# A new order for a whole kernel: retention with SwiGLU on one core, the first chunk in an older order

## The chip, the cores and the metric

The kernel runs on one core of a Trainium2 chip. A core has TensorE (PE, matrix products; its weight loads are shown as PEld), VectorE (DVE), ScalarE (ACT), GpSimd (POOL) and SyncE (SP, which only issues DMAs here); each runs its own queue of instructions in order, and they wait for each other by semaphores. Times are device microseconds (us). The metric is the median time of several executions; a profile is taken of one of them.

## The reference

Two parts, one after the other. First a retention layer with a state that decays by a factor of its own in each head, over 4 batches, 8 heads, 768 positions and 64 dimensions per head; then RMS norm and a SwiGLU layer over the 3072 rows of 512 that come out.

```python
gamma = 1.0 - 2.0 ** (-5.0 - np.arange(H))
for t in range(S):
    state = gamma * state + einsum('bhd,bhe->bhde', k[:, :, t], v[:, :, t])
    y[:, :, t] = scale * einsum('bhd,bhde->bhe', q[:, :, t], state)
x = y.transpose(0, 2, 1, 3).reshape(B * S, H * D)
xn = x / sqrt(mean(x * x, -1) + 1e-06) * rms_g            # 3072 x 512
g = xn @ w_gate                                           # 512 x 1536
out = (g * sigmoid(g) * (xn @ w_val)) @ w_out             # 1536 x 512
```

Inputs and output are float32; the kernel computes in bfloat16 with float32 sums.

## The kernel before

The 768 positions are six chunks (c = 0 to 5) of 128; a chunk has four batches (b = 0 to 3). For each (c, b) the retention is: load q, k, v; transpose q and k; scores by two groups of products, for the even and the odd heads (`A`, line 414); multiply each half by a decay mask on VectorE (`M0`, `M1`, line 437); products with v, and from chunk 1 on with the state as well (`Y`, lines 452 and 456); squares summed on ScalarE (`S`, line 469); 1/rms on GpSimd, two instructions (`R`, lines 479 and 481: ms and rstd); the norm on VectorE (`N`, line 493); transposition of the normed rows into xnT, by TensorE and a copy (`X`, `XE`) in chunks 0 and 1 and by a DMA from SyncE (`XE` on S) later. The state of the next chunk is made by `D` (k times decay, line 528, chunks 0 and 1), `K` (products, line 537), `U` (sum, line 545, or copy) and `B` (two casts on GpSimd, line 552).

The feed-forward part takes the four batches of a chunk together, 512 columns of xnT: for each 128 of the 1536 hidden columns `g` and `v` (line 560, four products each, into one bank of PSUM each), `s` (silu on ScalarE, line 570) and `h` (their product on VectorE, line 582). In chunk 0 the first of these are cut by batch: `g.0.2.3.0.3` is chunk 0, hidden block 2 to 3, batches 0 to 3. The output product is done by seven products per chunk instead of eight: `a1`, `a6`, `a7`, `a4`, `b2`, `c5`, `c3` (line 656), with sums of hT made ahead of them (`z1` to `z4`, line 629, on VectorE or GpSimd), sums of w_out (`w1` to `w4`, line 614), partial results kept (`q1`, `q6`, `q7`) and added (`r1` to `r4`, line 679 or a copy at line 148), and stores (`s1` to `s4`, line 684).

Nothing of the order is left to a scheduler: a table of some 985 entries, `ORDER`, is read from first to last, and each entry issues one step.

```python
for w in ORDER.split():
    w, _, bk = w.partition("/")        # the PSUM banks it takes
    w, _, en = w.partition("@")        # the engine: D, A, P, S
    f, *a = w.split(".")               # the step and its chunk, batch, blocks
    F[f](ENG.get(en), [int(i) for i in bk], *map(int, a))
```

So an entry sets the engine, the banks and the place in that engine's queue; each engine runs its own entries in the order of the table, and runs ahead of the others as far as data and buffers allow.

Loads (`Lq`, `Lk`, `Lv`; line 313) on GpSimd (@P) turn float32 into bfloat16 on the way. Those of q and k of chunk 0 on GpSimd take eight rows of a head at a time (line 323) and are transposed by sixteen small products with the tile `pick` (`T`, line 377); all others take rows (line 325) and need four transposes (line 382). For the former, k in rows is got back by transposing once more (`J`, line 521). Loads on SyncE (@S) arrive as float32 and are copied or scaled (`Ck`, `Cq`, `V`), and from chunk 2 on q and k are transposed by DMAs from SyncE (`tq`, `tk`, line 398). All loads of chunk 2 wait for the transfer wo.8.12, the last third of w_out:

```python
        if c == 2:
            after(i, ("wo", 8))
```

Weights come in by pieces on GpSimd (`wg`, `wv`, line 334; `wo`, line 341): wv.4.6 is blocks 4 and 5 of w_val. Warm-up products on a tile of ones (`hot`, line 242; `H`, line 248, 512 wide) stand in the head. Constants are made there too: `iota` (row_m), `ident`, `pick`, the masks `mk0`, `mk1`, `vd`, `yd`, `yt` on ScalarE, `causal`, `mc`, and `rms`, `G`, `GE` for the norm's weights; `tab` loads ScalarE's table for silu.

Of the kernel before, what the change touches and what calls it, by code (L numbers as in the profile page):

```python
# [22 lines left out]
M1.0.1 M0.0.1 K.0.3/4 Y.0.0/7 S.0.0 Y.0.1/2 R.0.3 A.0.2/63 J.0.2/5 N.0.3 wv.0.2 wv.2.4 M0.0.2 K.0.1/0 M1.0.2 Y.0.2/1
wg.4.6 S.0.1 H.3/6 R.0.1 D.0.2@D K.0.2/3 R.0.0 N.0.0 N.0.1 Tk.1.1/5 U.0.1@A U.0.2@D X.0.3/0 U.0.3@A S.0.2 Lq.1.0@P
R.0.2 Tk.1.2/4 Lk.1.0@P mc.0@P Tq.1.2/7 tab Ek.1.1@A N.0.2 Tk.1.3/6 XE.0.3@A Ek.1.2@D Eq.1.2@D Lq.1.1@P X.0.1/2
X.0.0/3 Tq.1.3/5 XE.0.1@A X.0.2/1 g.0.0.4.3.4/0 A.1.2/47 g.0.0.2.1.2/2 XE.0.0@D Eq.1.3@D XE.0.2@A g.0.3.4.0.3/3
v.0.0.4.3.4/5 s.0.0.4.3.4 mc.1@P M1.1.2 v.0.3.4.0.3/1 M0.1.2 v.0.0.2.1.2/0 h.0.0.4.3.4 D.1.3@D v.0.2.3.0.3/7 Ek.1.3@A
A.1.3/64 s.0.0.2.1.2 h.0.0.2.1.2 g.0.0.2.2.3/2 s.0.3.4.0.3 h.0.3.4.0.3 M0.1.3 M1.1.3 g.0.0.2.0.1/3 s.0.0.2.0.1
g.0.2.3.0.3/5 Tk.1.0/0 Ek.1.0@D wv.4.6 s.0.2.3.0.3 h.0.2.3.0.3 v.0.0.2.0.1/1 Tq.1.0/6 g.0.5.6.0.3/3 s.0.5.6.0.3 B.0.2
Eq.1.0@D v.0.5.6.0.3/4 h.0.5.6.0.3 Tq.1.1/5 D.1.0@D Eq.1.1@D h.0.0.2.0.1 g.0.4.6.3.4/0 g.0.4.5.0.3/7 s.0.4.5.0.3  # L30
s.0.4.6.3.4 v.0.0.2.2.3/6 v.0.4.5.0.3/3 h.0.4.5.0.3 s.0.0.2.2.3 h.0.0.2.2.3 wg.9.12 wv.9.12 Lv.1.2@P g.0.9.10.0.4/4
D.1.2@P wg.6.9 B.0.3 A.1.0/5701 M1.1.0 Lv.1.0@P Lv.1.1@P Lv.1.3@P v.0.4.6.3.4/2 h.0.4.6.3.4 wo.0.4 v.0.10.11.0.4/3
M0.1.0 g.0.10.11.0.4/6 wo.4.8 Y.1.2/7 D.1.1@P s.0.9.10.0.4 S.1.2 v.0.9.10.0.4/4 s.0.10.11.0.4 g.0.7.8.0.4/2
s.0.7.8.0.4 z1.0.0@D M1.1.1 K.1.2/5 M0.1.1 h.0.9.10.0.4 B.0.1 B.0.0 wo.8.12 Lq.2.0@S R.1.2 N.1.2 Y.1.1/1 S.1.1 Y.1.0/0
S.1.0 h.0.10.11.0.4 R.1.1 K.1.1/6 U.1.1@D g.0.6.7.0.4/4 U.1.2@D Lq.2.3@S Lq.2.2@S Lk.2.3@S R.1.0 Lv.2.3@S Lk.2.0@S
Y.1.3/7 s.0.6.7.0.4 S.1.3 R.1.3 N.1.1 N.1.0 K.1.0/2 U.1.0@D wv.6.9 g.0.8.9.0.4/3 X.1.2/6 z2.0.0@P w1@P v.0.11.12.0.4/5
Cq.2.3@P X.1.1/4 X.1.0/1 z4.0.0@P g.0.11.12.0.4/0 K.1.3/2 XE.1.2@D Lk.2.2@S XE.1.1@A Cq.2.2@P Ck.2.3@P s.0.11.12.0.4
N.1.3 X.1.3/6 XE.1.0@D g.1.3.4.0.3/7 v.1.2.3.0.3/4 v.1.1.2.0.3/1 v.1.3.4.0.3/0 Cq.2.0@P XE.1.3@D h.0.11.12.0.4 tq.2.2
U.1.3@D s.1.3.4.0.3 h.1.3.4.0.3 g.1.9.10.0.4/6 g.1.0.4.3.4/5 v.1.9.10.0.4/2 s.1.9.10.0.4 h.1.9.10.0.4 g.1.2.3.0.3/7
v.0.6.7.0.4/0 h.0.6.7.0.4 g.1.6.7.0.4/6 s.0.8.9.0.4 g.1.1.2.0.3/2 v.0.7.8.0.4/3 Ck.2.2@P Lv.2.0@S s.1.2.3.0.3  # L40
h.1.2.3.0.3 tk.2.3 B.1.3 h.0.7.8.0.4 z1.0.1@D v.0.8.9.0.4/0 g.1.8.9.0.4/7 s.1.6.7.0.4 s.1.8.9.0.4 g.1.5.6.0.4/4
Lk.2.1@S tq.2.3 z3.0.0@D h.0.8.9.0.4 s.1.1.2.0.3 z2.0.1@D v.1.0.1.0.3/6 Ck.2.1@P h.1.1.2.0.3 z1.0.2@D z3.0.2@D
z2.0.2@D z3.0.1@P B.1.2 z4.0.2@D w2@D v.1.8.9.0.4/3 h.1.8.9.0.4 g.1.0.1.0.3/0 s.1.0.1.0.3 v.1.0.4.3.4/7 V.2.0@A
Ck.2.0@A tk.2.2 v.1.6.7.0.4/2 Lv.2.2@S g.1.4.5.0.4/1 h.1.0.1.0.3 w3@D v.1.4.5.0.4/0 h.1.6.7.0.4 s.1.0.4.3.4
h.1.0.4.3.4 s.1.4.5.0.4 s.1.5.6.0.4 g.1.7.8.0.4/3 v.1.5.6.0.4/6 h.1.5.6.0.4 Lq.2.1@S Cq.2.1@D h.1.4.5.0.4 s.1.7.8.0.4
v.1.7.8.0.4/5 h.1.7.8.0.4 a1.0.0.3/1 A.2.2/2743 q1.0@D M0.2.3 B.1.1 g.1.11.12.0.4/6 tq.2.0 Lk.3.2@S s.1.11.12.0.4
g.1.10.11.0.4/0 V.2.2@P K.2.2/5 tk.2.0 B.1.0 a6.0.0.3 tk.2.1 v.1.11.12.0.4/4 s.1.10.11.0.4 M1.2.3 V.2.3@D U.2.2@D
M0.2.2 Y.2.3/6 q6.0@A Ck.3.2@A tq.2.1 A.2.0/3052 S.2.3 Lv.3.3@S V.3.3@A z4.0.1@P w4@P M1.2.2 Y.2.2/7 B.2.2 R.2.3
h.1.11.12.0.4 a7.0.0.3 Lv.2.1@S V.2.1@P Lk.3.1@S M0.2.0 S.2.2 M0.2.1 M1.2.0 c5.0.0.3/4 Y.2.0/3 Lq.3.3@S R.2.2 S.2.0
v.1.10.11.0.4/5 M1.2.1 N.2.3 Y.2.1/0 Lq.3.0@S R.2.0 q7.0@A Lq.4.0@S Lk.3.3@S K.2.1/2 b2.0.0.3/6 a4.0.0.3 S.2.1 r4.0@A  # L50
XE.2.3@S Ck.3.1@D N.2.2 K.2.3/7 r2.0 c3.0.0.3 N.2.0 h.1.10.11.0.4 R.2.1 N.2.1 Cq.3.3@P U.2.3@D z1.1.1@P z2.1.1@D
z4.1.1@D r1.0 Lv.3.2@S U.2.1@D a1.1.0.3/3 XE.2.2@S B.2.1 XE.2.0@S XE.2.1@S z1.1.2@D V.3.2@D Cq.3.0@P K.2.0/5 U.2.0@D
# [674 lines left out]
```

## Time and profile before

| | |
|---|---|
| runs, us | 235.49, 237.01, 237.24 (median 237.01) |
| the profiled execution, us | 236.33; its span, from the first to the last instruction, 234.5 |
| mean granted clock of TensorE | 0.985 |
| PE busy | 223.9 us (95%), 2051 products |
| PEld, DVE, ACT, POOL busy | 140.2 (60%), 164.9 (70%), 91.7 (39%), 129.7 us (55%) |
| DMA | 33.5 MB, mean 143 GB/s |

Ends of products are modelled, so a busy TensorE may still have small gaps. Rows of a timeline give the start, the time taken, engine, line, operation, tiles, how many instructions were merged, and in brackets how long the engine idled before and what it waited for.

### The profile page before, as it was taken

What the parts mean: (1) busy time and instruction counts of PE and PEld (TensorE: products, weight loads), DVE (VectorE), ACT (ScalarE), POOL (GpSimd) and SP (SyncE); (2) the same over time, 40 slices, a digit from 0 to 9 for tenths busy, and PEclk for the clock granted to TensorE, in tenths of its full rate; (3) what the DMA queues carried; (4) which work ended last, traced back from release to release, by engine and by line L of the source; (5) the groups of instructions that cost most, each with busy time, mean ns of one, the idle gap of its engine ahead of it and who ended that gap; (6) DMA issues with size and microseconds to landing.
All of it is one profiled execution on the core that took longest, in us unless ns stands there. A gap on an engine that the chain in (4) does not pass through costs nothing.

```text
span 234.5 us, 5291 instructions
## 1 busy us (share of the span) xinstructions
PE 223.9 (95%) x2051; PEld 140.2 (60%) x2051; DVE 164.9 (70%) x311; ACT 91.7 (39%) x212; POOL 129.7 (55%) x192
## 2 busy tenths in 40 slices
...
GB/s 128 187 160 196 113 155 179 206 186 217 169 142 204 216 134 140 198 188 259 192 153 182 182 133 173 188 115 112 206 0 4 111 0 0 45 92 0 89 227 134
DMA packets 107274, 33.50 MB, mean 143 GB/s; under 512 B 93425, under 2 KB 107249, under 8 KB 107250
## 3 DMA queue, kind: packets, MB, share of 16 engines
...
HBM read 28.31 MB, written 6.29 MB: 148 GB/s over the span
## 4 chain that ended last, share of the span: by engine, by line
PE 71%; DMA 8%; DVE 6%; POOL 4%; SPq 2%; issue 2%; ACT 1%; ACTq 0%; POOLq 0%; DVEq 0%
PE g_ps L560 23%; PE v_ps L560 22%; PE a L656 10%; PE c L656 6%; DMA qf<-in_q_dram 5%; DVE am L437 3%; PE y_ps L452 2%; POOL qb L350 2%; PE b L656 2%; DMA kf<-in_k_dram 2%; PE y_ps L456 2%; PE a_ps L414 2%; SPq L398 2%; PE kv_ps L537 1%; DVE hT L582 1%
## 5 line engine op out<-in xcount | busy, mean ns | idle before, releaser
L570 ACT ACTIVATE sg<-g_ps 128x512 bf16<-128x512 f32 (+2 forms) x76 | 43.0, 574 | 84.6 <-PE g_ps L560 64.2
L582 DVE TENSOR_TENSOR hT<-sg,v_ps 128x512 bf16<-128x512 bf16 (+2 forms) x76 | 48.5, 653 | 34.2 <-PE v_ps L560 21.8
L560 PE MATMUL g_ps<-xnT,wg_b 128*128 128x512 bf16 (+2 forms) x344 | 71.0, 345 | 1.1 <-DVE hT L582 1.1
L560 PE MATMUL v_ps<-xnT,wv_b 128*128 128x512 bf16 (+2 forms) x344 | 70.4, 344 | 0.0
L560 PEld LDWEIGHTS <-wg_b 128*128 128x128 bf16 x344 | 30.0, 98 | 29.4 <-issue 1.7
L560 PEld LDWEIGHTS <-wv_b 128*128 128x128 bf16 x344 | 30.2, 98 | 27.0
L656 PEld LDWEIGHTS <-hT 128*128 128x128 bf16 x288 | 27.8, 98 | 5.8 <-issue 0.6
L656 PEld LDWEIGHTS <-z 128*128 128x128 bf16 x216 | 20.9, 98 | 3.3
L437 DVE TENSOR_TENSOR am<-a_ps,causal 128x512 bf16<-128x512 f32 x32 | 20.4, 679 | 1.8 <-PE a_ps L414 1.8
L469 ACT ACTIVATE xsq<-y_ps 128x512 bf16<-128x512 f32 x22 | 13.2, 598 | 19.7 <-PE y_ps L456 16.3
L552 POOL CAST st_b<-st_f 64x256 bf16<-64x256 f32 x40 | 17.2, 430 | 6.1 <-PE y_ps L456 2.8
L493 DVE SCALAR_TENSOR_TENSOR xn<-y_ps,rstd,g_bc 128x512 bf16<-128x512 f32 x22 | 16.1, 745 | 5.8 <-POOL rstd L481 5.7
L350 POOL TENSOR_TENSOR qb<-qf,ydec 128x512 bf16<-128x512 f32 x12 | 13.6, 1130 | 10.2 <-DMA qf<-in_q_dram 9.9
L656 PE MATMUL a<-wo_b,hT 128*128 128x256 bf16 x144 | 17.9, 273 | 0.1
L479 POOL TENSOR_SCALAR ms<-ssq 128x1 f32<-128x1 f32 x24 | 5.2, 217 | 22.7 <-ACT xsq L469 21.6
L629 POOL TENSOR_TENSOR z<-hT 128x512 bf16<-128x512 bf16 x4 | 4.8, 1198 | 22.2 <-DVE hT L582 22.2
L481 POOL TENSOR_TENSOR rstd<-ms,mhalf 128x1 f32<-128x1 f32 x24 | 13.3, 554 | 2.0
L629 POOL TENSOR_TENSOR hT<-hT 128x512 bf16<-128x512 bf16 x9 | 11.7, 1308 | 2.5 <-DVE z L629 2.3
L452 PE MATMUL y_ps<-vp,am 128*128 128x64 bf16 x176 | 9.6, 198 | 2.7 <-DVE am L437 2.2
L452 PEld LDWEIGHTS <-am 128*128 128x128 bf16 x176 | 7.8, 100 | 6.6 <-DVE am L437 2.6
L437 DVE TENSOR_TENSOR am<-a_ps,mask 128x512 bf16<-128x512 f32 x16 | 10.3, 682 | 1.9 <-POOL mask L293 1.3
L148 ACT COPY sn<-a 128x512 f32<-128x512 f32 x11 | 6.4, 586 | 13.2 <-PE a L656 13.1
...
## 6 DMA issues: line engine op xcount, KB each, us to landing
...
```

The source lines that it names most:

```text
L350: e.tensor_tensor(out=u["qb"], in0=u["qf"], in1=ydec[:, c, :, None].to_broadcast([128, H, D]), op=ALU.mult)
L437: DVE.tensor_tensor(out=u["am"][:, i], in0=u["a"][i], in1=m, op=ALU.mult)
L452: nc.tensor.matmul(y[:, h, :], u["am"][:, h % 2, h // 2, :], u["vp"][:, h, :], start=h == 0, stop=c == 0 and h == H - 1, skip_group_check= ...
L469: ACT.activation(xsq, flat(u["y"]), AF.Square, accum_out=u["ssq"])
L481: POOL.tensor_tensor(out=u["rstd"], in0=ms, in1=mhalf, op=ALU.pow)
L493: DVE.scalar_tensor_tensor(out=u["xn"], in0=flat(u["y"]), scalar=u["rstd"], in1=g_bc, op0=ALU.mult, op1=ALU.mult)
L552: POOL.tensor_copy(st_b[b][r, :, i * 64:i * 64 + 64], st_f[b][r])
L560: nc.tensor.matmul(p[:, (n - n0) * m:(n - n0 + 1) * m], W[w][0][:, s, n * 128:(n + 1) * 128], xnT[c][:, s, b0 * C:b1 * C], start=s == 0, s ...
L570: ACT.activation(sg[:, :cols], done["wg", c, n0, b0][:, :cols], AF.Silu)
L582: DVE.tensor_tensor(out=h_of(c, r)[:, i:i + n1 - n0, b0 * C:b1 * C], in0=sg, in1=p, op=ALU.mult)
L629: e.tensor_tensor(out=x, in0=a, in1=b, op=how)
L656: nc.tensor.matmul(done[x, c][:, q], left(i, c, r)[:, k, q * C:q * C + C], right(i)[:, r, k], start=first and q == r == k == 0, stop=r == ...
```

## The change

Only the table `ORDER` changes, but nearly all of it. The steps are the same, apart from warm-ups (`H.8` at the start; 20 products of 512 columns instead of 12) and one copy: k of (0, 2) is loaded by SyncE in rows, so that `Ck.0.2` casts it on VectorE and its transposition takes four products instead of sixteen. The cut of the products and the seven output products per chunk stay. 97 entries change their engine: 23 of the z's go from VectorE to GpSimd and 13 the other way (38 run on GpSimd in all, 28 before), and w1 and w4 leave GpSimd for VectorE.

The head and the end of the table:

```diff
-hot.2/0 hot.3/1 Lq.0.1@P rms.1@S H.3/2 Lk.0.1@P Lq.0.3@P iota G/3 Lk.0.3@P Lk.0.0@P H.1/4 H.1/5 ident Lq.0.0@P
-Lq.0.2@P pick mk1 Lk.0.2@P vd H.1/6 Lv.0.3@P Tq.0.1/7 GE@D yt Lv.0.1@P mk0 Lv.0.0@P H.2/1 H.1/0 Eq.0.1@D Tq.0.3/2
...
-z4.5.1@D s2.5@S r1.4 s1.4@S c3.4.0.3 a4.5.0.2 c3.5.0.2 a4.5.2.3.1 r4.5.1@A r3.4 s3.4@S s4.5.1@S
-a4.5.2.3.0 r4.5.0@D c3.5.2.3.1 c3.5.2.3.0 a4.4.0.3 s4.5.0@S r3.5.1 r3.5.0 s3.5.0@S s3.5.1@S r4.4@A s4.4@S
+H.8/0 yt Lk.0.2@S ident pick Ck.0.2@D vd Lk.1.1@S iota Tk.0.2/1 rms.1@S D.0.2@D Lk.0.0@P Lq.0.1@P H.3/2 Tk.0.0/3 H.1/4
+Tq.0.1/5 Ek.0.0@D mk1 hot.3/6 J.0.0/7 D.0.0@D mk0 Lq.0.0@P Lk.0.1@P Tq.0.0/0 Lq.0.2@P Eq.0.1@A Eq.0.0@A Tk.0.1/2
...
+z4.5.1@P c3.4.0.3 r3.4 a4.5.0.2 c3.5.0.2 s3.4@S r1.5 s1.5@S a4.5.2.3.0 a4.5.2.3.1 r4.5.0@A s4.5.0@S z4.5.2@P
+c3.5.2.3.1 r3.5.1 s3.5.1@S c3.5.2.3.0 r3.5.0 a4.4.0.3 s3.5.0@S r4.5.1@D s4.5.1@S r4.4@A s4.4@S
```

The first place is GpSimd's queue around the first weights. The rows begin, before, behind the loads of q, k and v of chunk 0; qb and kb here are loads of chunk 1, ms and rstd are one batch's 1/rms, in the order b = 3, 1, 0.

```order
L325 DMA kb<-in_k_dram 128x8x64 x2
L325 DMA qb<-in_q_dram 128x8x64 x2
L334 DMA wg_b<-in_moe_w_gate_dram 128x4x256 x2
L479 TENSOR_SCALAR ms<-ssq 128x1
L481 TENSOR_TENSOR rstd<-ms,mhalf 128x1
L334 DMA wv_b<-in_moe_w_val_dram 128x4x256 x2
L334 DMA wg_b<-in_moe_w_gate_dram 128x4x256
L479 TENSOR_SCALAR ms<-ssq 128x1
L481 TENSOR_TENSOR rstd<-ms,mhalf 128x1
```

Now three weight pieces and one load of chunk 1 stand ahead of these rows, right behind the loads of v. The rstd's are those of b = 0, 2, 1 and 3; the weights are wv.2.4, wg.4.6 and, last, wv.4.6; st_b is the state of b = 0 (`B.0.0`).

```order
L479 TENSOR_SCALAR ms<-ssq 128x1
L481 TENSOR_TENSOR rstd<-ms,mhalf 128x1
L334 DMA wv_b<-in_moe_w_val_dram 128x4x256
L479 TENSOR_SCALAR ms<-ssq 128x1
L481 TENSOR_TENSOR rstd<-ms,mhalf 128x1
L479 TENSOR_SCALAR ms<-ssq 128x1
L481 TENSOR_TENSOR rstd<-ms,mhalf 128x1
L552 CAST st_b_125<-st_f_121 64x4x64 x2
L334 DMA wg_b<-in_moe_w_gate_dram 128x4x256
L479 TENSOR_SCALAR ms<-ssq 128x1
L481 TENSOR_TENSOR rstd<-ms,mhalf 128x1
L334 DMA wv_b<-in_moe_w_val_dram 128x4x256
```

Three weight pieces have moved ahead of the first rstd and four loads of chunk 1 behind; wv.4.6 has moved from behind the chunk 1 loads and masks to directly behind the fourth rstd.

The second place is VectorE's queue from the first masked scores (`am`) to the first products with silu. Before:

```order
L528 TENSOR_TENSOR kd<-t_ps,vdec 128x512
L437 TENSOR_TENSOR am<-a_ps,mask_101 128x512
L528 TENSOR_TENSOR kd<-t_ps,vdec 128x512
L437 TENSOR_TENSOR am<-a_ps,mask_101 128x512 x3
L528 TENSOR_TENSOR kd<-t_ps,vdec 128x512
L437 TENSOR_TENSOR am<-a_ps,mask_101 128x512 x2
L493 SCALAR_TENSOR_TENSOR xn<-y_ps,rstd,g_bc 128x512
L437 TENSOR_TENSOR am<-a_ps,mask_101 128x512 x2
L528 TENSOR_TENSOR kd<-t_ps,vdec 128x512
L493 SCALAR_TENSOR_TENSOR xn<-y_ps,rstd,g_bc 128x512 x2
```

Now, from the copy of q of b = 2 on (kd is `D`, xn is `N`, xnT is `XE`, hT is `h`):

```order
L148 CAST qT<-t_ps 128x512
L437 TENSOR_TENSOR am<-a_ps,mask_101 128x512 x7
L493 SCALAR_TENSOR_TENSOR xn<-y_ps,rstd,g_bc 128x512
L437 TENSOR_TENSOR am<-a_ps,mask_101 128x512
L148 COPY xnT<-xt_ps 128x4x128
L493 SCALAR_TENSOR_TENSOR xn<-y_ps,rstd,g_bc 128x512 x2
L148 COPY xnT<-xt_ps 128x4x128
L528 TENSOR_TENSOR kd<-t_ps,vdec 128x512
L582 TENSOR_TENSOR hT<-sg,v_ps 128x2x128
L528 TENSOR_TENSOR kd<-t_ps,vdec 128x512
L582 TENSOR_TENSOR hT<-sg,v_ps 128x2x128
```

Seven masks stand together, the state's `D`s of b = 1 and 3 have moved behind three of the norms, and gated products follow before the fourth.

The third place is SyncE's queue at the loads of chunk 2. Before, from the first of them (qf_984 is q of b = 0; then q of 3 and 2, k of 3, v of 3, k of 0 and 2; later qf_1397 is q of b = 1):

```order
L325 DMA kf_1145<-in_k_dram 128x8x64
L398 DMA_TRANSPOSE qT_1186<-qb_1148 128x4x128
L325 DMA vf_1254<-in_v_dram 128x8x64
L398 DMA_TRANSPOSE kT_1259<-kb_1150 128x4x128
L325 DMA kf_1285<-in_k_dram 128x8x64
L398 DMA_TRANSPOSE qT_1287<-qb_1115 128x4x128
L398 DMA_TRANSPOSE kT_1356<-kb_1252 128x4x128
L325 DMA vf_1363<-in_v_dram 128x8x64
L325 DMA qf_1397<-in_q_dram 128x8x64
```

Now (k and q of b = 2, then of 3, then k of 0; qf_1257 is q of b = 1, qf_1394 q of b = 0):

```order
L325 DMA kf_1247<-in_k_dram 128x8x64
L398 DMA_TRANSPOSE kT_1249<-kb_1238 128x4x128
L398 DMA_TRANSPOSE qT_1253<-qb_1251 128x4x128
L325 DMA qf_1257<-in_q_dram 128x8x64
L398 DMA_TRANSPOSE qT_1285<-qb_1283 128x4x128
L325 DMA kf_1312<-in_k_dram 128x8x64
L398 DMA_TRANSPOSE kT_1381<-kb_1287 128x4x128
L325 DMA qf_1394<-in_q_dram 128x8x64
L325 DMA vf_1398<-in_v_dram 128x8x64
```

Five loads of chunk 2 stand ahead of the first transposing DMA instead of seven; the v's now come last, behind the q's.

159 lines of the change are left out of this document (79 added, 80 removed).

## The prediction

> **What bounds the kernel now.** I read the page first, then busy time by stage, then the timeline of the stages that are not full.
>
> ```profile
> PE 71%; DMA 8%; DVE 6%; POOL 4%; SPq 2%; issue 2%; ACT 1%; ACTq 0%; POOLq 0%; DVEq 0%
> ```
>
> TensorE carries 71% of the chain that ended last. Busy time by stage (start and end, length, then busy us of PE, PEld, DVE, ACT and POOL; the column behind them is the granted clock) shows where it is not full:
>
> ```profile
> 15.70:22.50 6.80, 5.94 (x65) 4.00 (x63) 5.12 (x9) 5.61 (x14) 6.25 (x13) 0.50 1.61 188
> 23.70:68.30 44.60, 44.60 (x432) 27.61 (x430) 33.09 (x61) 20.17 (x47) 34.67 (x48) 1.00 1.21 176
> 68.30:77.90 9.60, 8.29 (x101) 5.38 (x100) 7.50 (x12) 3.54 (x9) 6.76 (x7) 1.00 1.19 175
> 77.90:230.60 152.70, 150.94 (x1232) 95.08 (x1228) 107.35 (x186) 51.93 (x120) 66.18 (x97) 1.00 0.64 127
> ```
>
> From 23.7 us on TensorE stands still for 1.3 us in chunk 2 (68.3 to 77.9), for 1.8 us in the long rest up to 230.6, and then for the last copy and store. The feed-forward products are the same set in both orders, so the time can change in three ways only: how much real work TensorE has done when the head is over, the waits later, and the tail. The head first:
>
> ```profile
> 1.44 0.76 POOL L323 DMA_DIRECT2D qb<-in_q_dram  x1 [0.21 <-issue]
> 3.49 1.06 POOL L323 DMA_DIRECT2D kb<-in_k_dram  x2
> 6.59 2.75 POOL L325 DMA_DIRECT2D vp<-in_v_dram  x3
> 11.34 0.62 PE L414 MATMUL a_ps<-qT,kT 64*128 64x128 bf16 x16
> 12.60 1.88 DVE L437 TENSOR_TENSOR am<-a_ps,mask 128x512 bf16<-128x512 f32 x3
> 13.90 1.56 POOL L334 DMA_DIRECT2D wg_b<-in_moe_w_gate_dram  x2
> 19.65 0.19 POOL L479 TENSOR_SCALAR ms<-ssq 128x1 f32<-128x1 f32 x1
> 19.93 0.55 POOL L481 TENSOR_TENSOR rstd<-ms,mhalf 128x1 f32<-128x1 f32 x1
> 20.51 1.41 DVE L493 SCALAR_TENSOR_TENSOR xn<-y_ps,rstd,g_bc 128x512 bf16<-128x512 f32 x2 [1.11 <-POOL rstd L481]
> 23.70 1.06 PE L560 MATMUL g_ps<-xnT,wg_b 128*128 128x128 bf16 x16
> ```
>
> GpSimd issues the loads one after the other, VectorE multiplies eight score halves by their masks, and its norms wait for GpSimd's rstd, which stands behind weight loads. So the first feed-forward product starts at 23.70 us. Products before that are short, and warm-ups among them.
>
> **The change, step by step.** First the head, walked with the durations above.
>
> ```profile
> 3.24 0.33 POOL L252 TENSOR_SCALAR_AFFINE_SELECT row_m<-row_f 128x128 f32<-128x128 f32 x1
> 9.92 0.44 PE L377 MATMUL t_ps<-pick,qb 128*64 128x64 bf16 x16
> DMA to landing us min/median/max: 4.3/5.0/5.2
> ```
>
> (The last line is that of the tile kb over the first 60 us.)
>
> Three constants of this size (0.33 or less) now precede the loads, less the 0.2 that GpSimd idles there now: the first load is issued at 2.2 us instead of 1.44. At 0.76 for the first and 0.53 for each next, k.0.1, the fourth load, is issued at 4.0 and lands 5.0 later, at 9.0. Its sixteen small transposes (0.44), ScalarE's copy of them (0.6, as its square of the same size below) and two more groups on TensorE give the scores of b = 0 and 1 at about 10.6, against 11.34 now. The load of k.0.2 that went to SyncE takes no time of the path; its four transposes at J.0.2 make a tile that nothing reads (0.22 us of TensorE). The eight extra 512-wide warm-ups all lie ahead of the first product, where TensorE waits anyway; if the loads came earlier, each would cost 0.2 us at full clock.
>
> VectorE then takes one copy (0.7, as a norm) and seven masks in a row; three last 1.88 now, so 0.63 each: from 11.35 to 15.75. The D's that stood among the masks go ahead of the scores or behind the first norms. The first norm needs rstd:
>
> ```profile
> 20.21 1.28 ACT L298 ACT_TABLE_LOAD   x1
> 13.76 0.60 ACT L469 ACTIVATE xsq<-y_ps 128x512 bf16<-128x512 f32 x1 [2.77 <-PE y_ps L452]
> 14.25 0.19 ACT L469 ACTIVATION_READ_ACCUMULATOR xsq<-y_ps 128x1 f32 x1
> 23.92 0.42 DVE L148 COPY xnT<-xt_ps 128x512 bf16<-128x512 bf16 x1
> ```
>
> ScalarE is done with k.0.1's copy at 10.55; ydec, the table load (1.28; with the two small operations beside it an estimate of 1.8) and three copies (0.6) stand ahead of the squares (0.79) of b = 0, which end at 14.95. GpSimd has by then issued all it can (2.2 + 0.76 + 6 x 0.53 + 5 x 0.92 + 3 x 0.78 = 13.1) and waits, with every later weight queued behind; rstd takes 0.83 (19.65 to 20.48 above) and is there at 15.8. VectorE's norm (0.7) ends at 16.5, an eighth mask at 17.3, the copy to xnT (0.42) at 17.7: with its place behind Y.0.3, the first product starts near **18.1** us instead of 23.70.
>
> TensorE's queue from there is priced by these rows (the last is GpSimd's, for B.0.0):
>
> ```profile
> 23.86 0.89 PE g_ps L560 x16
> 121.69 2.59 PE g_ps L560 x12
> 23.42 0.22 PE t_ps L382 x4
> 24.76 0.33 PE a_ps L414 x8
> L552 POOL CAST st_b<-st_f 64x256 bf16<-64x256 f32 x40 | 17.2, 430 | 6.1 <-PE y_ps L456 2.8 <-DVE st_f L545 2.0
> ```
>
> It holds six groups of eight 128-wide products (6 x 0.45), two groups of four 384-wide (2 x 0.65, at 3/4 of 2.59/12), three K's (priced as a group of transposes, 0.2) and five groups of four transposes (5 x 0.22): 5.7 us, and 0.5 for the second and third norm. It arrives at v.0.4.5.0.3 at 24.3. That product needs wv.4.6, which GpSimd issues behind all four rstd's, in order: rstd 0 until 15.8, wv.2.4 (0.78) 16.6, rstd 2 17.4, rstd 1 18.2, B.0.0 (two casts of 0.43) 19.0, wg.4.6 19.8, rstd 3 20.6. Landing:
>
> ```profile
> DMA to landing us min/median/max: 4.9/4.9/4.9
> ...
> DMA to landing us min/median/max: 5.8/6.0/6.3
> ```
>
> The first line is that of the one load of wv_b that had no other weights just ahead of it (at 26.2 us), the second that of the two at 16.4 and 17.2, in a row. So wv.4.6 lands between 25.5 and 26.9; I take **26.0**, nearer the lone one, since a rstd stands between it and wg.4.6. TensorE loses 1.7 of its 5.6 us there: all its products stand behind the waiting one, and VectorE's gating products behind them. At that moment it has done 6 x 0.45 + 2 x 0.65 of feed-forward and one transpose group of chunk 1, 4.2 us. Before, at 23.70 + 0.89 + 0.33 + 0.45 + 0.65 = 26.0, it has these (three groups of products and one score) and five transpose groups of chunk 1, 3.4 us. All else of chunk 0 is done in both. The head gives **-0.9** (bounds -2.6 with no wait, 0 with the late landing).
>
> Next, chunk 1. X.1.3 stands 3.7 us of products behind Y.1.3; squares, rstd, norm (0.79 + 0.83 + 0.7), the end of Y.1.3 (0.4) and two ScalarE copies queued ahead (1.2) need 3.9 and more. Before there are 4.2 us between and nothing is lost. I take **+0.5** (0 to +1).
>
> Chunk 2 is where 1.3 us stand still now:
>
> ```profile
> 39.98 0.81 POOL L341 DMA_DIRECT2D wo_b<-in_moe_w_out_dram  x1
> 60.06 1.20 SPq L398 DMA_TRANSPOSE kT<-kb  x1
> 49.49 2.27 SPq L325 DMA_DIRECT2D qf<-in_q_dram  x3
> 65.18 0.57 SPq L325 DMA_DIRECT2D qf<-in_q_dram  x1
> 70.49 0.77 DVE L350 TENSOR_TENSOR qb<-qf,ydec 128x512 bf16<-128x512 f32 x1 [2.10 <-DMA qf<-in_q_dram]
> 71.92 1.02 PE L560 MATMUL g_ps<-xnT,wg_b 128*128 128x512 bf16 x4 [0.63 <-DVE hT L582]
> 75.93 0.41 PE L452 MATMUL y_ps<-vp,am 128*128 128x64 bf16 x8 [0.47 <-DVE vp L369]
> ```
>
> SyncE's loads start when wo.8.12, issued at 39.98, has landed, at 49.49. The last q is issued at 65.18, behind four transposing DMAs, and VectorE, in order, waits 2.10 us for it with gating products of chunk 1 behind; TensorE pays at 71.92 and 75.93. In the new order GpSimd has, from wv.4.6 at 20.6 up to wo.8.12, six weights (0.78), ten loads (0.92), three B's (0.87) and three mask constants (2.6, priced as z's below): 39.7, so the start is the same. SyncE's first transposing DMA waits for GpSimd's copy of k.2.2, behind a z that needs VectorE's z1.0.1, some 28.5 us of products after 26.0: 54.9 + 1.2 + 0.6 = 57. Behind that DMA and one more (1.2 each) q.2.1 is issued near 59.5 and lands near 65. VectorE comes to it 37 us of products after 26.0 with the half us of chunk 1 on top, at 63.7: a wait of 1.2 instead of 2.1. The last q, q.2.0, is wanted near 69 and there. I take **-0.9** for TensorE's share of the shorter wait and of the late V (0 to -2.2).
>
> The tail:
>
> ```profile
> 228.46 0.38 PE L656 MATMUL a<-w,hT 128*128 128x256 bf16 x2 [0.46 <-ACT r L148]
> ```
>
> The halves of a4.5.2.3 share a bank, and the copy of one stood between them. Now they follow each other: **-0.46**, nothing behind it changes.
>
> Ten more of the z's run on GpSimd, and two w's less:
>
> ```profile
> L629 POOL TENSOR_TENSOR z<-z,hT 128x512 bf16<-128x512 bf16 x7 | 8.1, 1156 | 1.2 <-DVE z L629 1.0
> L629 DVE TENSOR_TENSOR z<-z,hT 128x512 bf16<-128x512 bf16 x11 | 5.6, 506 | 0.3 <-POOL z L629 0.2
> ```
>
> They cost 1.2 us there for 0.5 on VectorE; TensorE's products cover both, and the last ones (z4.5.1, z4.5.2) end by these prices some 3 us before their product, so nothing (0 to +0.5, if that cover is short).
>
> Sum: -0.9 + 0.5 - 0.9 - 0.46 = -1.76, say **-1.7**. The profiled execution took 236.33 us (span 234.5 and 1.8 around it): 234.6. It lies 0.7 below the median of the runs, 237.01, so I predict **235.3** us for a median.
>
> **Rivals.** *A, the weights are in time.* If wv.4.6 is issued by 19.5 (no wait for rstd 3 as walked) the 1.7 us of waiting go, the head gives -2.6 and the total 233.6. For it: 4.9 was measured. Against it: rstd 3 hangs on the eighth mask, and the order on GpSimd is fixed.
>
> *B, SyncE blocks in chunk 2: slower.* Its first transposing DMA now stands ahead of q.2.1, q.2.0 and all four V's, and waits for k.2.2's copy, which stands behind three z's of 1.2 us on GpSimd. Each us by which that copy comes after 57 is a us more of waiting at VectorE for q.2.1, and the V's of the chunk come later too. If it comes at 60.5, VectorE waits 4.7 (57 gave 1.2) instead of 2.1; TensorE pays 2.6 more instead of 0.9 less, and the total is 238.8. It decides against the forecast's gain from about 58.8 on. Against it: in the stretch 23.70 to 68.30 GpSimd was busy 34.7 of 44.6 us, so that it has some room, and its rstd's of chunk 1 are the only other things it waits for there.
>
> *C, the clock.* Between 15.70 and 22.50 the granted clock was 0.50 and cost little, since TensorE had no feed-forward work. In the new order real products start at 18.1; at half clock until 22.5 they are 2.2 us late, of which the wait for wv.4.6 hides 1.7. If the half clock held half as long again as those 6.8 us, until 25.9, another 1.7 us are lost, this time in the open: total 237.5. [...]
>
> *D, the change does nothing*, since TensorE is full from 24 us on in both: 237.0. That is near what the sum gives with all its terms at their weak end.
>
> **How the numbers follow.** Forecast 0.50 (its own spread 236.4 to 234.0), A 0.22, B 0.14, C 0.08, D 0.06. One per cent, about what a measurement of this kernel can tell from no change, is 2.4 us: faster below 234.6, slower above 239.4. Faster: most of A and a third of the forecast, 0.36. Slower: half of B and some mishap, 0.12. Same: 0.52. The range reaches from below A's 233.6 by its own uncertainty (the full 2.2 of chunk 2 on top of it) to B's 238.8: 232.0 to 238.8.
>
> **What would show it.** The first product with wg_b near 18 us; a wait of TensorE for wv_b near 24 to 26 us, and wv.4.6 issued near 20.6; VectorE's wait for qf in chunk 2 near 1 us; no wait for r at the end. The prediction is wrong if the first products come after 20 us (masks or squares late), if TensorE waits again between 26 and 50 us, or if the transposing DMAs of chunks 3 to 5, which I only followed by their places in SyncE's queue, come late.

## The result

The changed kernel takes 234.23 us (median of 20 runs, 232.39 to 239.7), the kernel before 237.22 (20 runs): a ratio of 0.9879, with a 95% interval of 0.9852 to 0.9907. The forecast was 235.3 us, 1.7 under the 237.01 known then; the median fell by 3.0. The profiled executions, though, are 236.33 and 234.66 us (spans 234.5 and 233.0), 1.67 apart.

Where those 1.67 us come from is read best from **time lost along TensorE's list**: for each entry of the table, the start of its first weight load less the full-clock durations of all products listed ahead of it. Where the number grows, TensorE stood still or ran at half clock. The numbers are of one execution of each kernel. The new list is 1.55 us longer (1.72 of warm-ups more, four transposes for sixteen small products); its numbers below have that added, so that the columns compare real work.

| TensorE's list at | before | changed | change in the stretch (minus: gained) | forecast |
|---|---|---|---|---|
| 35 us (head) | 11.24 | 10.54 | -0.70 | -0.9 |
| 65 us (chunk 1) | 11.73 | 10.92 | -0.11 | +0.5 |
| 85 us (chunk 2) | 14.18 | 11.80 | -1.57 | -0.9 |
| 130 us (chunk 3) | 15.92 | 13.22 | -0.32 | 0 |
| 200 us (chunks 4, 5) | 17.73 | 16.22 | +1.19 | 0 |
| last product (tail) | 18.45 | 17.00 | +0.06 | -0.46 |

The sum of the stretches is -1.45, and the spans differ by 1.5. The page of the changed kernel shows none of this: TensorE's share of the chain fell from 71% to 60%, and its busy share stays 95%.

```profile
PE 60%; DMA 13%; POOL 12%; SPq 5%; DVE 3%; issue 3%; ACT 2%; POOLq 0%; DVEq 0%; ACTq 0%
```

The head, in the timeline:

```profile
18.13 0.61 PE L560 MATMUL g_ps<-xnT,wg_b 128*128 128x128 bf16 x8
19.35 0.81 POOL L334 DMA_DIRECT2D wg_b<-in_moe_w_gate_dram  x1
21.02 0.81 POOL L334 DMA_DIRECT2D wv_b<-in_moe_w_val_dram  x1
26.43 0.82 PE L560 MATMUL v_ps<-xnT,wv_b 128*128 128x384 bf16 x4 [2.20 <-DMA wv_b<-in_moe_w_val_dram]
```

The first feed-forward product starts at 18.13 us (forecast 18.1). wv.4.6 is issued at 21.02 (20.6), TensorE waits 2.20 us for it and starts v.0.4.5.0.3 at 26.43 (26.0). That is within 0.5 us of the prediction's walk, but in an execution with a half clock in its head; one without it follows below. Busy time by stage (start and end, length, busy us of PE, PEld, DVE, ACT, POOL, then the granted clock and two columns on DMA) shows the half clock and the wait:

```profile
11.50:14.60 3.10, 3.10 (x51) 2.01 (x51) 2.13 (x5) 2.24 (x6) 1.69 (x4) 0.50 1.95 172
24.20:26.40 2.20, 0.02 (x1) 0.00 (x0) 0.14 (x1) 0.98 (x2) 2.20 (x4) 1.00 1.51 136
```

The half clock has moved: before it held from 15.70 to 22.50 us, now from 11.5 to 14.6, ahead of the feed-forward products. VectorE's masks then wait for the scores:

```profile
13.94 1.29 DVE L437 TENSOR_TENSOR am<-a_ps,mask 128x512 bf16<-128x512 f32 x2 [0.97 <-PE a_ps L414]
```

Chunk 2, SyncE and VectorE:

```profile
56.58 1.30 SPq L398 DMA_TRANSPOSE kT<-kb  x1
59.24 0.57 SPq L325 DMA_DIRECT2D qf<-in_q_dram  x1
62.62 0.75 DVE L350 TENSOR_TENSOR qb<-qf,ydec 128x512 bf16<-128x512 f32 x1
```

The first transposing DMA goes at 56.58 (forecast 57), q of batch 1 is issued at 59.24 (59.5), and VectorE takes it at 62.62 without a wait in its row, where 1.2 us were forecast and 2.10 stood before. So this load had landed 3.4 us after its issue at the latest; the walk had counted 5.5. (The next q, issued at 63.11, landed in 3.8.)

Chunk 4, where time is given back, in GpSimd's, TensorE's and SyncE's rows:

```profile
142.61 0.61 POOL L148 CAST kb<-kf 128x512 bf16<-128x512 f32 x1
143.16 0.85 POOL L552 CAST st_b<-st_f 64x256 bf16<-64x256 f32 x2
143.56 1.22 SPq L398 DMA_TRANSPOSE kT<-kb  x1
145.18 0.55 POOL L481 TENSOR_TENSOR rstd<-ms,mhalf 128x1 f32<-128x1 f32 x1
148.15 0.71 PE L537 MATMUL kv_ps<-vp,kb 128*64 128x64 bf16 x16 [0.66 <-DVE xn L490]
164.49 0.38 PE L456 MATMUL y_ps<-st_b,qT 128*128 128x128 bf16 x4 [0.56 <-POOL st_b L552]
```

The squares of batch 3 are ready at 140.5, but GpSimd first does two V's, a copy of k and two state casts, so that the first rstd comes at 145.7; TensorE's K.4.0 needs a bank which the norms behind it release. The second wait, for the state casts B.4.2, stands behind two z's on GpSimd. In the kernel before, K.4.0 stands ahead of chunk 4's norms (the second half of the first row), the first rstd comes with no V or cast put ahead of it, and the state products of Y.5.2 follow without a wait:

```profile
119.84 0.44 PE L537 MATMUL kv_ps<-vp,kb 128*64 128x64 bf16 x16
147.22 0.55 POOL L481 TENSOR_TENSOR rstd<-ms,mhalf 128x1 f32<-128x1 f32 x1
168.55 0.39 PE L456 MATMUL y_ps<-st_b,qT 128*128 128x128 bf16 x4
```

The tail:

```profile
227.45 0.38 PE L656 MATMUL c<-wo_b,z 128*128 128x256 bf16 x2 [0.52 <-DVE r L679]
```

The wait of 0.46 us for the copy of a4.5.2.3 is gone, and one of 0.52 for the sum r3.5.1 has come: the halves of c3.5.2.3 share a bank too, and in the new order a sum stands between them.

### The profile page after: what moved, and what is told of

Read it like the earlier page. It is cut to its first block, busy times and chain, and to the rows that moved or that the text cites. A ratio compares the mean times of both kernels' runs of the same rounds, so it can differ in the third digit from the quotient of the medians.

```text
span 233.0 us, 5251 instructions
## 1 busy us (share of the span) xinstructions
PE 220.5 (95%) x2024; PEld 139.4 (60%) x2047; DVE 161.1 (69%) x299; ACT 89.7 (39%) x199; POOL 139.4 (60%) x203
## 4 chain that ended last, share of the span: by engine, by line
PE 60%; DMA 13%; POOL 12%; SPq 5%; DVE 3%; issue 3%; ACT 2%; POOLq 0%; DVEq 0%; ACTq 0%
PE v_ps L560 18%; PE g_ps L560 17%; PE a L656 9%; PE c L656 5%; DMA vf<-in_v_dram 4%; DMA qf<-in_q_dram 3%; POOL z L629 3%; DMA wv_b<-in_moe_w_val_dram 2%; PE b L656 2%; DMA kb<-in_k_dram 2%; DMA kf<-in_k_dram 2%; SPq L325 2%; PE a_ps L414 2%; POOL vp L369 2%; PE y_ps L452 2%
## 5 line engine op out<-in xcount | busy, mean ns | idle before, releaser
L570 ACT ACTIVATE sg<-g_ps 128x512 bf16<-128x512 f32 (+2 forms) x76 | 42.4, 574 | 82.0 <-PE g_ps L560 67.3
L560 PE MATMUL g_ps<-xnT,wg_b 128*128 128x512 bf16 (+2 forms) x331 | 68.7, 343 | 0.9 <-DVE am L437 0.2
L560 PEld LDWEIGHTS <-wg_b 128*128 128x128 bf16 x344 | 30.4, 98 | 27.7 <-issue 0.3
L629 POOL TENSOR_TENSOR z<-hT 128x512 bf16<-128x512 bf16 x10 | 11.6, 1162 | 22.5 <-DVE hT L582 22.4
L552 POOL CAST st_b<-st_f 64x256 bf16<-64x256 f32 x40 | 18.4, 461 | 2.7 <-DVE st_f L545 1.4
L369 POOL TENSOR_TENSOR vp<-vf,vdec 128x512 bf16<-128x512 f32 x10 | 11.4, 1144 | 13.8 <-DMA vf<-in_v_dram 13.8
L148 ACT COPY sn<-a 128x512 f32<-128x512 f32 x14 | 8.2, 585 | 25.1 <-PE a L656 25.1
L350 POOL TENSOR_TENSOR qb<-qf,ydec 128x512 bf16<-128x512 f32 x9 | 9.5, 1062 | 10.9 <-DMA qf<-in_q_dram 10.8
L629 POOL TENSOR_TENSOR z<-z,hT 128x512 bf16<-128x512 bf16 x11 | 13.3, 1213 | 1.3 <-DVE z L629 0.7
L629 POOL TENSOR_TENSOR z<-hT,z 128x512 bf16<-128x512 bf16 x8 | 9.3, 1161 | 3.4 <-PE a L656 2.8
L679 DVE TENSOR_TENSOR r<-c,sn 128x512 f32<-128x512 f32 (+1 forms) x13 | 8.4, 644 | 3.9 <-PE c L656 2.4
```

What stands on the lines that cost most here:

```text
L350: e.tensor_tensor(out=u["qb"], in0=u["qf"], in1=ydec[:, c, :, None].to_broadcast([128, H, D]), op=ALU.mult)
L369: e.tensor_tensor(out=u["vp"], in0=u["vf"], in1=vdec[:, c, :, None].to_broadcast([128, H, D]), op=ALU.mult)
L552: POOL.tensor_copy(st_b[b][r, :, i * 64:i * 64 + 64], st_f[b][r])
L560: nc.tensor.matmul(p[:, (n - n0) * m:(n - n0 + 1) * m], W[w][0][:, s, n * 128:(n + 1) * 128], xnT[c][:, s, b0 * C:b1 * C], start=s == 0, s ...
L570: ACT.activation(sg[:, :cols], done["wg", c, n0, b0][:, :cols], AF.Silu)
L629: e.tensor_tensor(out=x, in0=a, in1=b, op=how)
```

## The experiments

### The wait for wv.4.6, and the clock

The first weight piece behind the first rstd, wv.2.4, is not used until 29 us, the last, wv.4.6, at 24. They were exchanged:

```diff
-... X.0.0/4 J.0.3/6 wv.2.4 S.0.1 ... v.0.0.2.0.1/1 X.0.1/4 wv.4.6 causal ...
+... X.0.0/4 J.0.3/6 wv.4.6 S.0.1 ... v.0.0.2.0.1/1 X.0.1/4 wv.2.4 causal ...
```

> The changed kernel with two weight pieces exchanged in GpSimd's queue: wv.4.6 is issued where wv.2.4 was (15.0 us) and wv.2.4 where wv.4.6 was (21.0 us). In the changed kernel TensorE waits 2.2 us for wv.4.6 at 24.2 us, while wv.2.4 is first needed at 29.0. Theory 'queue place' (the wait is only the place of that load in GpSimd's queue, and what TensorE gains there it keeps): wv.4.6 lands near 20.5, no wait for wv_b at 24 us, the product v.0.3.4 finds wv.2.4 landed at 26.5, and the total falls by 2.2 us, from 234.2 to about 232.0 as a median. Rival 'something else is late next' (VectorE's norms and copies, or the loads of chunk 1, take the place of the wait): total falls by less than 0.7 us.

Measured: 232.07 us, ratio to the kernel before 0.9806 (0.9767 to 0.9845). TensorE's row has no wait:

```profile
23.41 0.39 PE L506 MATMUL xt_ps<-ident,xn 128*128 128x128 bf16 x4
23.63 0.81 PE L560 MATMUL v_ps<-xnT,wv_b 128*128 128x384 bf16 x4
```

The wait is gone, nothing took its place in the trace, and the medians lie 2.2 us apart, as the first theory said (1.8, when each is set against the kernel before that ran beside it). How much of that is the wait and how much the clock is taken up below. Rival A of the prediction ("the weights are in time") named this term rightly; its price there was 1.7.

The changed kernel was run again beside the rest of this group:

> The changed kernel, unaltered, timed once more beside the three that follow. Expected 234.2 us as before (233.5 to 235.0). In its executions so far the mean granted clock is either about 1.0 (median 233.4) or about 0.993 (median 234.9).

Measured: 234.45 us, ratio 0.9883 (0.9833 to 0.9934). Its profiled execution had no half clock between 6.4 and 231 us and took 232.1 us:

```profile
11.50:14.60 3.10, 3.10 (x71) 1.93 (x72) 3.08 (x6) 2.15 (x5) 2.06 (x4) 1.00 1.94 173
16.77 0.61 PE L560 MATMUL g_ps<-xnT,wg_b 128*128 128x128 bf16 x8
19.70 0.81 POOL L334 DMA_DIRECT2D wv_b<-in_moe_w_val_dram  x1
24.68 0.82 PE L560 MATMUL v_ps<-xnT,wv_b 128*128 128x384 bf16 x4 [1.81 <-DMA wv_b<-in_moe_w_val_dram]
```

The masks run without a gap, the first product starts at 16.77 instead of 18.13, and the head is worth 2.31 us at 35 us instead of 0.70 (8.93 lost, against 11.24). So one kernel has two heads. Not all of the difference between these two is the clock: in the eight profiles of kernels with these warm-ups and no half clock in the head the first product came at 16.6 to 17.8 us, in the two with one at 18.1 and 18.7. Over both sets of its runs, those with a mean granted clock of 0.996 or more have a median of 233.37 us (12), those below it 234.72 (11, without the three longest; 235.17 with them): at least 1.35 apart. In the kernel before the same split gives 236.70 (26) and 236.99 (37): the half clock of its profile, from 15.7 to 22.5 us, lies ahead of its first feed-forward product at 23.70. The clock is also a part of why the first pair of profiles lies only 1.67 us apart and the medians 3.0: the changed kernel's profile, with half clock, is 0.4 above its median; the other 0.9 is that the profile of the kernel before lies that much under its own.

This bears on the exchange of wv.4.6 too. All six of its executions had a mean clock of 0.997 or more; against the changed kernel's executions at 0.996 or more its gain is 1.3 us, not 2.2. And the two full-clock profiles end alike (span 230.6 us with the exchange, 230.4 without), though v.0.4.5.0.3 starts at 23.63 instead of 24.68. What the wait costs apart from the clock is therefore not fixed by these runs: between nothing and some 1.3 us.

Without the eight warm-ups at the start (H.8/0 taken out):

> The changed kernel without the eight 512-wide warm-up products at its start. Theory 'they are free and do nothing' (TensorE waits for its first k until 4.6 us anyway): total within 0.5 us of the changed kernel's 234.2, the granted clock in the head as there. Rival 'they keep the clock up': without them the clock of the first products is lower or half for longer, the first feed-forward product comes later than 18.1 us and the total is 0.7 us or more above 234.2.

Measured: 236.77 us, ratio 0.9988 (0.9961 to 1.0015): all of the gain is gone. Stages of it:

```profile
4.00:22.00 18.00, 17.41 (x292) 11.89 (x293) 14.32 (x27) 13.43 (x36) 15.76 (x27) 1.00 1.51 165
22.00:25.60 3.60, 1.51 (x36) 1.19 (x33) 1.44 (x4) 1.99 (x4) 3.60 (x6) 1.00 1.38 118
25.60:29.20 3.60, 3.60 (x31) 3.24 (x32) 0.69 (x1) 0.43 (x1) 3.60 (x5) 0.57 1.32 138
```

The rival was right that they matter, but not in the way it said: the first product comes no later than in other profiles at full clock, at 17.40 us, and from 4 to 22 us the clock is full. The half clock now comes behind the wait for wv.4.6, when nothing covers it: the time lost goes from 9.93 to 11.52 between v.0.4.5 and v.0.3.4. That is 1.6 us; the medians are 2.5 apart, and where the rest goes was not followed up. Of its twelve executions none had a mean clock of 0.998 or more.

Is it the warm-ups, or the wait for wv.4.6, behind which the half clock stood? Both were taken away, the warm-ups and the wait:

> The changed kernel with the weight pieces exchanged (no wait for wv.4.6 at 24 us) and without the eight warm-up products at the start. Without the eight alone the kernel took 236.8 us, and its trace showed the clock at half behind the wait for wv.4.6. Theory 'the idle wait brings the half clock': with no wait there is no half clock in the open, and the total is that of the exchange alone, 232.1 us, within 0.7. Rival 'the warm-ups are worth 2.5 us by themselves' : about 234.6.

Measured: 233.35 us, ratio 0.9855 (0.9811 to 0.9898), all six executions at a clock of 0.997 or more. So the half clock at this place went when the wait did, as the first theory said: over all profiles of kernels with this head, one stood directly behind the wait in four of the eight that have the wait (waits of 2.1 to 2.8 us), and in none of the four in which it is taken away or filled. But the total lies 1.3 above that of the exchange alone, half way to the rival's. The profile has it not in the head (7.48 lost at 30 us on the list's common terms, 7.99 with warm-ups) but from chunk 2 on, 0.55 more at 85 us and 0.78 more at 200.

Last, nine dummy products of 512 columns, on bank 7, were put ahead of v.0.4.5.0.3, to keep TensorE busy through the wait:

> The changed kernel with nine 512-wide products on the tile of ones (1.9 us at full clock) directly ahead of v.0.4.5.0.3, where TensorE waits 2.2 us for wv.4.6 in any case. Theory 'the idle wait brings the half clock': filled, the wait starts no half clock behind it, the total is 0.5 to 1.5 us under the changed kernel run beside it, and the low-clock executions of it are gone. Rival 'clock and wait have nothing to do with each other': within 0.3 us of the changed kernel or slower.

Measured: 234.84 us, ratio 0.9905 (0.9871 to 0.994). The clock did what was expected (0.996 or more in eleven of twelve executions), the time did not: no gain on the changed kernel beside it, as the rival said. Its profiled execution waits elsewhere, in chunks 2 and 3:

```profile
76.76 0.39 PE L452 MATMUL y_ps<-vp,am 128*128 128x64 bf16 x8 [1.03 <-POOL vp L369]
114.44 1.47 PE L656 MATMUL c<-w,z 128*128 128x256 bf16 x12 [1.70 <-DVE xn L493]
```

The first of these waits (0.7 to 1.0 us) stands in three of the other profiles too, those of both runs without warm-ups and of the last run below, and is missing in those of the changed kernel, of the exchange and of the tail. V.2.2, which it waits for, stands on GpSimd behind z1.1.1, which came behind it before. Why it is late in some profiles only stays open, and so does what a half clock behind the wait is worth by itself.

### The head alone

The changed order for its first 178 entries (first chunk), then the remaining entries in the order of the kernel before:

```diff
 ... g.0.9.10.0.4/6 s.0.9.10.0.4 A.1.2/45 Tk.1.0/3
-mc.0@P Lv.1.1@P Lv.1.0@P v.0.11.12.0.4/2 ...
+Lk.1.3@P Lk.4.2@S Lq.1.3@P mc.0@P Tk.1.3/6 Tq.1.3/1 ...
```

> The changed kernel's order for the first 178 entries (first chunk: its loads, transposes, masks, norms, first feed-forward products), and behind them all remaining entries in the order of the kernel before (one bank renumbered where the two don't fit). Theory 'head is worth less than 1 us' (the first product starts 5.6 us earlier, but TensorE then waits 2.2 us and has done less of the retention; by 35 us the changed kernel is 0.7 us ahead): total 0.7 us under the kernel before (0.2 to 1.2). Rival 'the whole gain is the head's' : total 2.9 us under the kernel before. Rival 'the head is worth nothing without its sequel': within 0.2 us of the kernel before.

Measured: 240.87 us, ratio 1.0178 (1.0139 to 1.0218), slower than either kernel; none of the three cases expected it. TensorE's rows behind the seam:

```profile
38.52 0.40 PE L382 MATMUL t_ps<-ident,kb 128*128 128x128 bf16 x4 [1.75 <-DMA kb<-in_k_dram]
39.35 0.40 PE L382 MATMUL t_ps<-ident,qb 128*128 128x128 bf16 x4 [0.44 <-DMA qb<-in_q_dram]
43.94 1.03 PE L414 MATMUL a_ps<-qT,kT 64*128 64x128 bf16 x16 [1.63 <-DVE kT L148]
```

The new head puts weights ahead of loads of chunk 1; the old rest wants those loads at once. In the new order feed-forward products stand ahead of chunk 1's transposes, so that these loads have more time there. The waits are not all of it: behind them the clock is at half for 6.7 us, of which TensorE is busy 4.74, so that some 2.4 us of the loss are the clock's.

```profile
41.40:48.10 6.70, 4.74 (x41) 2.83 (x41) 5.30 (x10) 0.35 (x1) 0.38 (x1) 0.50 1.19 188
```

A seam at 410 entries, behind the retention of chunk 2, was to tell what chunks 4 and 5 give back:

> The changed kernel's order for its first 410 entries (until the products of chunk 2's retention are issued), then the remaining entries in the order of the kernel before (six banks renumbered). By the time lost along TensorE's list the changed kernel is 2.4 us ahead at 85 us and ends 1.5 ahead. Theory 'the new order of chunks 4 and 5 gives 0.9 back' : this kernel loses 4.3 us behind 85 us like the kernel before and not 5.2, and ends 2.4 us under the kernel before in its profile, about 0.9 under the changed one. Rival 'what is gained early is lost late whatever the order' (later limits by DMA or VectorE): ends like the changed kernel, 234.2, or worse.

Measured: 243.57 us, ratio 1.0277 (1.0236 to 1.0317). Up to 85 us it follows the changed kernel (12.75 lost, 11.80 there); then the seam costs 10 us, in waits like these and in a half clock from 94.1 to 100.9 us:

```profile
94.05 0.43 PE L537 MATMUL kv_ps<-vp,kb 128*64 128x64 bf16 x8 [4.12 <-ACT kb L148]
98.03 1.87 PE L560 MATMUL v_ps<-xnT,wv_b 128*128 128x512 bf16 x4 [3.55 <-DMA xnT<-xn]
```

It says nothing on chunks 4 and 5, since TensorE comes to them 10 us later. At 260 entries the two tables have done the same steps but for 13 on either side:

> The changed kernel's order for its first 260 entries (first chunk, and the retention of chunk 1), then the remaining entries in the order of the kernel before; at this place the two tables have done the same steps but for three or four, so that the seam is clean. Theory 'head and chunk 1 are worth 0.8 us' (time lost along TensorE's list at 65 us): 0.8 us under the kernel before (0.2 to 1.5). Rival 'the seam costs again' (loads put off by the new head are wanted by the old rest): slower than the kernel before. Rival 'the head is most of the 2.9 us': 2 us or more under it.

Measured: 237.8 us, ratio 1.0013 (0.998 to 1.0045): no gain, and the theory fell. Stages of it, and one row:

```profile
23.00:26.20 3.20, 0.66 (x16) 0.45 (x8) 0.78 (x3) 1.33 (x3) 3.20 (x5) 1.00 1.44 133
26.20:30.00 3.80, 3.69 (x37) 3.43 (x38) 0.69 (x1) 0.60 (x1) 3.80 (x5) 0.67 1.74 169
54.17 0.40 PE L506 MATMUL xt_ps<-ident,xn 128*128 128x128 bf16 x4 [1.26 <-DVE xn L493]
```

Here the half clock falls behind the wait for wv.4.6, as without warm-ups, and all twelve executions have one somewhere (mean clock 0.986 to 0.993), though the head's entries are those of the changed kernel. The list is at 11.97 at 35 us, 0.7 behind the kernel before instead of 0.7 ahead; then X.1.3, which has 1.3 us of products between Y.1.3 and itself here and 3.2 in the changed kernel, costs a wait of the kind that the prediction had feared, and chunk 2 loses 2.2 as before. So the worth of this head depends in large part on where the clock drops: +0.7, -0.7 and -2.3 us at 35 us in three executions.

### Chunk 2

In the kernel before, one load was moved ahead, q of batch 1:

```diff
-... h.0.11.12.0.4 tq.2.2 ... h.1.5.6.0.4 Lq.2.1@S Cq.2.1@D ...
+... h.0.11.12.0.4 Lq.2.1@S tq.2.2 ... h.1.5.6.0.4 Cq.2.1@D ...
```

> The kernel before with one load moved: q of batch 1 of chunk 2 (Lq.2.1) is issued by SyncE ahead of its first transposing DMA instead of behind four of them, as the changed order has it in spirit. Theory 'one late q' (the 2.4 us that the kernel before loses between 68 and 85 us, against 0.6 in the changed one, come from VectorE's wait of 2.1 us for this q and from what stands behind it): the wait goes, TensorE loses 1.2 us less or better in chunk 2, total 1.2 to 1.9 us under the kernel before. Rival 'the whole order of chunk 2': the copy that comes earlier does not help, since the late V of batch 3 and the masks hold TensorE as long: total within 0.5 us of the kernel before.

Measured: 235.66 us, ratio 0.9953 (0.9933 to 0.9973), 1.1 us under the kernel before, just short of the 1.2 to 1.9 expected. VectorE takes the q without waiting:

```profile
56.37 1.33 SPq L325 DMA_DIRECT2D qf<-in_q_dram  x1
68.54 0.80 DVE L350 TENSOR_TENSOR qb<-qf,ydec 128x512 bf16<-128x512 f32 x1
99.64 1.02 PE L560 MATMUL g_ps<-xnT,wg_b 128*128 128x512 bf16 x4 [1.15 <-DVE hT L582]
```

Between 65 and 85 us it loses 0.88 instead of 2.45, a gain of 1.57, the same as the changed kernel has there: chunk 2's term is this one load and what stood behind it on VectorE. Some of it is given back at 99.64, where TensorE waits 1.15 for hT (0.47 before).

### Chunk 4 and the tail

GpSimd's order was altered where the changed kernel waits in chunks 4 and 5:

```diff
-... S.4.2 Ck.5.3@P tk.5.2 a1.2.0.3/7 Lq.5.0@S B.3.1 V.5.3@D b2.2.0.3/4 R.4.3 tk.5.3 Lv.5.2@S R.4.2 ...
+... S.4.2 R.4.3 B.3.1 R.4.2 Ck.5.3@P tk.5.2 a1.2.0.3/7 Lq.5.0@S V.5.3@D b2.2.0.3/4 tk.5.3 Lv.5.2@S ...
-... z1.3.0@P z3.3.0@P S.5.3 B.4.2 Y.5.2/6 ...
+... B.4.2 z1.3.0@P z3.3.0@P S.5.3 Y.5.2/6 ...
```

> The changed kernel with GpSimd's order altered in two places: in chunk 4 the two 1/rms of batches 3 and 2 (R.4.3, R.4.2) and the state casts B.3.1 stand ahead of the copy Ck.5.3, and B.4.2 stands ahead of the sums z1.3.0 and z3.3.0. Theory 'GpSimd is late' (the changed kernel loses 1.04 us at K.4.0, which waits for a bank that the norms of chunk 4 release behind those 1/rms, and 0.86 us behind Y.5.2, which waits for B.4.2): both waits go, total down by 1.0 to 1.9 us. Rival 'given back' (the copies and sums put off are then late for their own readers, or TensorE waits for the next thing): total down by less than 0.5 us.

Measured: 236.88 us, ratio 0.9993 (0.9958 to 1.0028). The two waits went (K.4.0 loses 0.31 instead of 1.04, nothing behind Y.5.2), and a larger one came. SyncE and TensorE:

```profile
147.96 1.20 SPq L398 DMA_TRANSPOSE kT<-kb  x1
154.43 4.56 SPq L512 DMA_TRANSPOSE xnT<-xn  x3
160.36 1.02 PE L560 MATMUL g_ps<-xnT,wg_b 128*128 128x512 bf16 x4 [1.99 <-DMA xnT<-xn]
```

The copy Ck.5.3, put off on GpSimd, is what SyncE's tk.5.3 waits for; it goes at 147.96 instead of 143.56, with the transposing DMAs of chunk 4's norms queued behind it. "Given back" was right, and by more than it said. (Its profile also has a half clock from 27.1 to 30.4 us, behind the wait for wv.4.6.)

The halves of c3.5.2.3 were put together, ahead of r3.5.1:

> The changed kernel with the two halves of c3.5.2.3, which share a bank, next to each other instead of with a copy between them. Theory 'the stall only moved' (the change took away a wait of 0.46 us for a copy at the end and made one of 0.5 to 0.7 us for the sum r3.5.1): no wait of TensorE in the last 5 us, total down by 0.6 us. Rival 'the last store sets the end' (the copies and stores of the last products are queued behind one another whatever TensorE does): total unchanged.

Measured: 233.96 us, ratio 0.9866 (0.9818 to 0.9914), 0.3 us under the changed kernel and not to be told from it. In the trace the wait of 0.52 us is gone, and the last twelve products follow without a gap:

```profile
226.83 0.60 PE L656 MATMUL c<-wo_b,z 128*128 128x256 bf16 x4
227.27 1.47 PE L656 MATMUL a<-w,hT 128*128 128x256 bf16 x12
```

All together, with Ck.5.3 on ScalarE, which has time there (busy 3.78 of the 8 us from 140 to 148 in the changed kernel, GpSimd 7.43), so that SyncE is not held up (against the run with GpSimd's order altered):

```diff
-... S.4.2 R.4.3 B.3.1 R.4.2 Ck.5.3@P tk.5.2 ...
+... S.4.2 R.4.3 B.3.1 R.4.2 Ck.5.3@A tk.5.2 ...
```

> The changed kernel with the weight pieces exchanged (minus 2.2 measured alone), the two halves of c3.5.2.3 together (minus 0.3 measured, its stall of 0.68 gone in the trace), and GpSimd's order of chunk 4 as in the run where R.4.3, R.4.2 and B.3.1 stand ahead, but with the copy Ck.5.3 on ScalarE in its old place of time, so that SyncE's transposing DMA of it is not held up. Theory 'GpSimd's copy was what SyncE stood behind': the 2.2 us of waiting for the transposed norms of chunk 4 that the earlier run showed are gone, K.4.0 and Y.5.2 wait under 0.4 us, total 234.2 - 2.2 - 0.5 - 1.5 = 230.0 us (229.4 to 231.0). Rival 'chunk 4 gives it back in any order': 231.6.

Measured: 230.78 us, ratio 0.9743 (0.9702 to 0.9784), the fastest of all. K.4.0 comes behind the products ahead of it without a wait,

```profile
146.07 1.47 PE L656 MATMUL a<-w,z 128*128 128x256 bf16 x12
147.47 0.55 PE L537 MATMUL kv_ps<-vp,kb 128*64 128x64 bf16 x16
```

and neither the wait for chunk 4's transposed norms nor that of the tail is in its trace, though the profiled execution was one with half clock in the head (12.3 to 15.6 us). Between 130 and 200 us its list loses some 1.6 us less than the changed kernel's. So what chunk 4 gave back belonged to this order of GpSimd's queue and not to a limit behind it.

## Why the prediction was right, and where its steps were off

The measured 234.23 lies in the range, 1.1 under the forecast of 235.3. The sum was close for the execution that was profiled (-1.76 worked out, -1.67 measured), in part by luck: of its four terms the two of chunks 1 and 2 were of the wrong size and that of the tail did not come about, the head's holds for only one kind of execution, and a term for chunks 4 and 5 was missing.

- **Head, forecast -0.9, measured -0.7 in the first profile and -2.3 in the second.** The queues and the wait came as walked: 18.1 against 18.13 us for the first product, 20.6 against 21.02 for the issue of wv.4.6, a wait of 1.7 against 2.2. That the times agree so well is partly luck: the first profile has a half clock that the walk had not counted, and at full clock the first two come at 16.77 and 19.70, 0.9 to 1.3 earlier, with a wait of 1.81. (The work that the prediction lists, 4.2 against 3.4 us, gives -0.8, not -0.9.) What failed is that the half clock of the kernel before (15.7 to 22.5 us) was treated as a feature of the place, with a loss only if it stayed there (rival C, chance 0.08). It moved (11.5 to 14.6 us), and it differs from execution to execution: 14 of 26 have a mean clock under 0.996, with a median that is 1.35 us or more longer. The half clock until 22.5 or 25.9 us that rival C priced did not come: in the first profile it was over by 15 us, and the second had none in the head.
- **Warm-ups, put at nothing.** "Ahead of the first product, where TensorE waits anyway" left out the clock: without them two of twelve executions have a mean clock of 0.996 or more, against 12 of 26 with them, and the kernel takes 236.77 us; without them and the wait, at 0.997 or more in all six, it takes 1.3 more than without the wait alone.
- **Chunk 1, forecast +0.5, measured -0.1.** The norm of batch 3 was ready at 52.8 us and X.1.3 came at 53.17. The term that was wrong is the 1.2 us of "two ScalarE copies queued ahead": ScalarE idled for 1.39 us and took the squares as soon as Y.1.3 was done. The wait is real where fewer products stand ahead of X.1.3 (1.26 us in the run with the seam at 260).
- **Chunk 2, forecast -0.9, measured -1.57.** The queue walk held (56.58 and 59.24 us against 57 and 59.5), and rival B, which needed the first transposing DMA after 58.8, did not come. The mis-sized term is the rest of VectorE's wait: 1.2 was left, and there was none, since the load took at most 3.4 us to land and not 5.5. One load moved in the kernel before gives the same 1.57 us, so the mechanism is shown.
- **Chunks 4 and 5, not in the sum, measured +1.2.** The prediction named as a risk the transposing DMAs it had only followed by their places; the loss came on GpSimd instead, whose V's, copies and z's stand ahead of rstd's and state casts. The step that failed is the pricing of what moved to GpSimd at nothing ("TensorE's products cover both"): it asked when a z's own product comes, and not what is queued behind the z.
- **Tail, forecast -0.46, measured +0.06.** "Nothing behind it changes" was wrong: c3.5.2.3, also in one bank, had been cut in two by a sum in the same lines.

Rival D, no change, is out by the interval. That the total was so near is in part the cancelling of chunk 2 against chunk 4. The 0.3 us gained in chunk 3 were neither forecast nor followed up.
